# Attention and spectral mixing on one core: where x is added, and how far z runs ahead of u in the last loop

## The chip, the core and the metric

The kernel runs on one core of one Trainium2 chip. The metric is the device time of one execution in microseconds (us). A profile of one execution on the chip stands beside the times. PE is the matrix engine (PEld its weight loads), DVE the vector engine, ACT the scalar engine, POOL the GpSimd engine, SP the engine that here only issues DMAs.

## The reference

Two stages. The first is causal attention with a decay bias, for batch 8, 8 heads, sequence 576, head size 64:

```
scores = q k^T / 8 + min(-(cum_i - cum_j), 0), causal      cum = cumsum(max(s, 0))
attn   = softmax(scores);   x = attn v                      x: 8 x 576 x 512
```

The second mixes x in frequency, with 64 modes, each with its own 512 x 512 complex matrix:

```
X = rfft(x over the sequence)[:64];   Y = X (w_r + i w_i) per mode;   y = irfft(Y)
u = x + y;   z = u w_ch;   out = u + max(z, 0)              out: 8 x 576 x 512, float32
```

The mode matrices are 134 MB in float32. They are most of what the kernel reads.

## The kernel before, in words

**Schedule.** The instructions of each engine run in the order in which the program writes them (`manual_schedule`); semaphores for data and for the reuse of buffers are put in by the framework.

**First part.** A loop over 32 steps (4 groups of two heads, 8 batches) does attention, the forward transform of x and, beside it, the products with the mode matrices of group after group (128 input columns each). The mode matrices stream in by DMAs that POOL issues (line 225), 256 KB each, into two rings of buffers, throughout. The modes are cut into eight chunks of eight; `modes(g, c)` (line 443) multiplies chunk c of group g and adds it to `y_acc`.

**Last group.** After the loop the chunks of group 3 come one by one (lines 775 to 808), each making the final rows of Y for its modes. For each chunk the rows are transposed (`y_transposed`), multiplied by w_ch (`y_times_wch`), and spread over `yv`, which holds Y and Y w_ch for all chunks: chunks 0 to 3 and 4 to 5 by `gather`, chunks 6 and 7 by DMAs on SP's queue (`spread`). With `yv` there, u and z of a block of 128 rows are small matmuls with the inverse transform G: u = x + G Y and z = x w_ch + G (Y w_ch).

**Pairs.** The output goes out in 18 pairs of blocks of 128 rows by 512 columns: 16 pairs are two neighbouring blocks of one batch, and pairs 4 and 10 are tails, the last 64 rows of four batches each. x w_ch of a pair takes 8 transposes on PE (`x_transposed`, line 606), two copies on DVE and 8 matmuls (`x_times_wch`, line 618). For pairs 2 to 17 it is worked out beforehand and kept in SBUF, in one of three ways (`ways`, "esesvsesvsesvses" for pairs 2 to 17):

- "e": two float16 parts, put into z by four matmuls with the identity on PE (line 845);
- "s": float32, copied into z's PSUM buffer by ACT (line 841);
- "v": float32, added to z by DVE at the end (line 761).

Pairs 0 and 1 (`NPRE = 2`) have their x w_ch made between chunks 4 and 5 and left in z's PSUM buffers. While chunk 7 is multiplied, `modes` calls `first_u` and `first_z` between its parts: they open u of pair 0 and z of pairs 0 and 1 with the chunks that are done. When chunk 7 is there, its own part is added (`add_last`), relu is taken, and pair 1's u is made.

**Last loop.** For pair i of 2 to 17, in this order: `pre(i)` adds G (Y w_ch) into z (two matmuls of 512 columns, after the four of way "e"); `start_u(i)` puts x into u's PSUM by two matmuls with the identity (line 732); `add_y` adds G Y (two matmuls, line 713); ACT seeds z of the next pair where its way is "s"; `relu(i)` on ACT (line 751, 1024 columns); `finish(i)` adds u and relu on DVE, one add of 512 columns for each block (line 766; for way "v" lines 761 and 762), and SP issues one output DMA for each block (line 768; in tails one for 64 rows).

**PSUM.** z has two buffers of two banks. u alternates between `upool` (even pairs) and `auxpool` (odd pairs), two buffers of one bank in each.

Of the kernel before, what the change touches and what calls it, by code (L numbers as in the profile page):

```python
# [9 lines left out]
FP32 = mybir.dt.float32  # L10
# [8 lines left out]
def kernel(  # L19
# [11 lines left out]
    nc = tc.nc  # L31
# [74 lines left out]
    wpool = ctx.enter_context(tc.tile_pool(name="w_sb", bufs=WA))  # L106
    wpool2 = ctx.enter_context(tc.tile_pool(name="w2_sb", bufs=WB))
    spool = ctx.enter_context(tc.tile_pool(name="small_sb", bufs=2))
    auxpool = ctx.enter_context(tc.tile_pool(name="aux_psum", bufs=2, space=PSUM))

    at = ExitStack()
    ap_ = at.enter_context(tc.tile_pool(name="attn", bufs=1))
# [330 lines left out]
    def modes(g, c, meanwhile=None):  # L443


        ps = auxpool.tile([P, DM], FP32, name="yp", tag="aux")
        cols = xs[g % 2].rearrange("p q k h r b m -> p q k (h r b) m")

        def product(ri, q_, cg):
            k0 = HP if ri == 1 and c == 0 and cg == 0 else 0  # L450
            nc.tensor.matmul(  # L451
                ps[32 * cg : 32 * cg + 32, :],
                cols[k0:, q_, 1 - ri, :, c * MC // 2 + cg],
                wt[(g, c, ri, cg // 2)][k0:, 2 * (cg % 2) + q_, :],
                start=(ri == 0 and q_ == 0), stop=(ri == 1 and q_ == 1),
                tile_position=(k0, 32 * cg), skip_group_check=True,
            )

        for x in range(4):
            ri, y = divmod(x, 2)  # L460
            if meanwhile and x in meanwhile:
                meanwhile[x]()
            for z in range(4):
                if meanwhile:
                    product(ri, z // 2, 2 * y + z % 2)
                else:
                    product(ri, y, z)
        if g == 0:
            nc.vector.tensor_copy(out=y_acc[:, c, :], in_=ps)
# [22 lines left out]
    for i, b in ((4, 0), (10, B // 2)):  # L492
        pairs.insert(i, ((b, NF), (b + 2, NF)))
    NPRE = 2
    kept = list(range(NPRE, len(pairs)))


# [83 lines left out]
    Gx_sb = finpool.tile([P, NX, NF * P], FP16, name="Gx_sb")  # L581
    nc.vector.memset(Gx_sb.rearrange("p c t -> p (c t)").bitcast(FP32), 0.0)
    nc.sync.dma_start(out=Gx_sb[0:P:B], in_=d_Gx)
    upool = ctx.enter_context(tc.tile_pool(name="u_psum", bufs=2, space=PSUM))
    zpool = ctx.enter_context(tc.tile_pool(name="z_psum", bufs=2, space=PSUM))

    NLOC = 5
    old = xs_flat[0]
# [11 lines left out]
    def parts(b, T):  # L600

        if T < NF:
            return [(slice(0, P), b, ident16h)]
        return [(slice(NL * i, NL * i + NL), b + i, ident16h[:NL, :NL]) for i in range(2)]

    def x_transposed(i):
        xts[i] = xt_sb[len(xts) % 2]
        for x, (b, T) in enumerate(pairs[i]):
            ps = upool.tile([P, DT, P], FP32, name="xt_ps", tag="u")
            for rows, bb, ident in parts(b, T):  # L610
                for dt in range(DT):
# [92 lines left out]
    order_z = list(late)  # L704
    TAKE = (3, 2, 4, 0, 0, 0)
    us, rs = {}, {}
    GK = P - 2 * MC * NX

    def add_y(dst, i, which, rows=slice(0, P), start=False):
# [9 lines left out]
    def add_last(dst, i, yb, cols=slice(0, DM), c=NX - 1):  # L719

        for x, (b, T) in enumerate(pairs[i]):
            nc.tensor.matmul(
                dst[x][:, cols], Gx_sb[:, c, bass.ts(T, P)], yb[:, cols],
                start=False, stop=True, skip_group_check=True,
            )

    def start_u(i):
        pool, tag = ((upool, "u"), (auxpool, "aux"))[i % 2]
        us[i] = [pool.tile([P, DM], FP32, name="u_ps", tag=tag) for x in range(2)]
        for x, (b, T) in enumerate(pairs[i]):  # L730
            for r, bb, ident in parts(b, T):
                nc.tensor.matmul(  # L732
                    us[i][x][r, :].rearrange("p (g d) -> p g d", d=P), ident,
                    x_all[: r.stop - r.start, :, bb, T, :],
                    start=True, stop=False, skip_group_check=True, tile_position=(0, r.start),
                )

    def result(i):

        if i % 2 == 0 or i == len(pairs) - 1:  # L740
            return finpool.tile([P, 4 * DM], BF16, name="r_sb", tag="r", bufs=3).bitcast(FP32).rearrange(
                "p (x e) -> p x e", x=2
            )
        t = wpool.tile([P, WM, DM], BF16, name="r_w", tag="w")
        return t.rearrange("p m e -> p (m e)").bitcast(FP32).rearrange("p (x e) -> p x e", x=2)
# [6 lines left out]
                out=rs[i][:, n * x : n * x + n], in_=zs[i][:, n * x : n * x + n], func=ACTF.Relu  # L752
            )

    def finish(i):
        if ways.get(i) == "v":
            rs[i] = result(i)
        for x, (b, T) in enumerate(pairs[i]):
            o = rs[i][:, x, :]
            if ways.get(i) == "v":  # L760
                nc.vector.tensor_tensor(out=o, in0=zs[i][:, x, :], in1=z1s[i][:, x, :], op=ALU.add)
                nc.vector.scalar_tensor_tensor(
                    out=o, in0=o, scalar=0.0, in1=us[i][x], op0=ALU.max, op1=ALU.add
                )
            else:
                nc.vector.tensor_tensor(out=o, in0=us[i][x], in1=o, op=ALU.add)
            for r, bb, _ in parts(b, T):
                nc.sync.dma_start(
                    out=out[bb, bass.ds(T * P, r.stop - r.start), :], in_=rs[i][r, x, :]
                )  # L770

    def z_of(i):
        return [zs[i][:, x, :] for x in range(2)]
# [1 line left out]
    for c in range(NCK - 2):  # L775
        yb = modes(NG - 1, c)
        for x in range(TAKE[c] - 1):
            work()
        if c >= NY:
            x_transposed(c - NY)  # L780
        yt = y_transposed(yb, c)
        if TAKE[c]:
            work()
        if c >= NY:
            x_times_wch(c - NY, False)
            y_times_wch(c, yt)
            if c == NCK - 3:
                gather(NY, NCK - 2, (), (0,))
        elif c == NY - 1:
            gather(0, NY, (1, 3), (1, 0))  # L790
    assert not order_z and not ahead
    c = NCK - 2
    yb6 = modes(NG - 1, c)
    yt = y_transposed(yb6)
    vb6 = y_times_wch(c, yt)


    def first_u():
        start_u(0)
        add_y(us[0], 0, 0, slice(0, GK))  # L800
        add_last(us[0], 0, yb6, c=0)

    def first_z():
        for i in range(NPRE):
            add_y(z_of(i), i, 1, slice(0, GK))
            add_last(z_of(i), i, vb6, c=0)

    yb = modes(NG - 1, NCK - 1, {2: first_u, 3: first_z})

    yt = spool.tile([P, DT, P], FP16, name="yt_sb", tag="yt")  # L810
    for x in range(2):
# [2 lines left out]
        for dt in range(dts.start, dts.stop):  # L814
            nc.tensor.transpose(ps[:, dt - dts.start, :], yb[:, bass.ts(dt, P)], ident16h)
        nc.scalar.copy(out=yt[:, dts], in_=ps)
    add_last(us[0], 0, yb)
    vb = spool.tile([P, DM], FP16, name="v_sb", tag="v")
    for cols in halves:
        vp = auxpool.tile([P, DM // 2], FP32, name="v_ps", tag="aux")  # L820
        for dt in range(DT):
            nc.tensor.matmul(
                vp, yt[:, dt, :], wch_sb[:, dt, cols], start=(dt == 0), stop=(dt == DT - 1)
            )
        nc.vector.tensor_copy(out=vb[:, cols], in_=vp)
    spread(NCK - 1, 1, vb)
    for i in range(NPRE):
        for cols in halves:
            add_last(z_of(i), i, vb, cols)
        relu(i, 2 - i)  # L830
    start_u(1)
    add_y(us[1], 1, 0, slice(0, GK))
    add_last(us[1], 1, yb6, c=0)
    add_last(us[1], 1, yb)


    def seed(i):
# [17 lines left out]
            zs[i] = zpool.tile([P, 2, DM], FP32, name="z_ps", tag="z")  # L855
        add_y(z_of(i), i, 1, start=ways[i] == "v")

    if ways[NPRE] == "s":
        seed(NPRE)
    for i in range(NPRE):  # L860
        finish(i)
    last = len(pairs) - 1
    for i in range(NPRE, len(pairs)):
        pre(i)
        start_u(i)
        add_y(us[i], i, 0)
        if ways.get(i + 1) == "s":
            seed(i + 1)
        if ways[i] != "v":
            relu(i, 2 if i == last else 1)  # L870
        finish(i)


# [28 lines left out]
```

## Time and profile before

| | |
|---|---|
| median of 8 runs | 450.99 us (449.75 to 451.75) |
| the profiled execution | 449.75 us, span 447.9 us |
| mean granted PE clock | 0.892 |
| busy in the span: PE, DVE, ACT, POOL | 355.4, 257.3, 222.1, 241.8 us |
| DMA | 93.31 MB, 81.29 of it from POOL's queue |
| last two DVE adds of the loop | from 443.39 on, 1.28 us |

The span is from the first to the last instruction. Matmuls are pipelined: their ends are modelled, and PE being busy doesn't mean that it is at its peak. Shares of the whole span average over stages with different limits; the weight stream runs for the first nine tenths, the last loop has the last thirty microseconds or so.

### The profile page before, as it was taken

Reading aid. Unit: us, or ns where it says so; the run is one execution under the profiler, and the core shown is the slowest. Engines: PE = TensorE matmul, PEld = TensorE weight load, DVE = VectorE, ACT = ScalarE, POOL = GpSimd, SP = SyncE. Lnnn points to the kernel's source line nnn. Section 1 sums busy time; section 2 is a strip of 40 time slices with the busy share of each in tenths; the row PEclk is TensorE's granted clock in tenths of the full one; section 3 lists DMA queues with packets and bytes.
Section 4 is the critical chain, followed back from the end, with each engine's and each line's share of the span. In section 5 each row is a group of like instructions: output and inputs, shape, how many; then the busy total and the mean of one; then the engine's idle time right before and its main releaser. Section 6 shows DMA issues by size and latency. Waiting matters only on the chain.

```text
span 447.9 us, 11548 instructions
## 1 busy us (share of the span) xinstructions
PE 355.4 (79%) x4713; PEld 225.0 (50%) x4745; DVE 257.3 (57%) x599; ACT 222.1 (50%) x390; POOL 241.8 (54%) x397
## 2 busy tenths in 40 slices
PE   1789988996555989854979688789897996859995
PEld 1456666564333656633546455556564555423332
DVE  7774776675333566733446545546665565542796
ACT  1584778466233656733436443555650434231774
POOL 7866666755566666555666665566554444430000
PEclk9995999999678899969659966779997999988999
DMA  9999999999999999999999999999999999994688
GB/s 182 199 204 206 204 203 205 206 206 206 208 207 202 202 189 200 208 207 207 204 203 206 207 205 206 208 205 199 208 209 211 210 209 210 209 217 102 236 303 315
DMA packets 77540, 93.31 MB, mean 208 GB/s; under 512 B 30432, under 2 KB 40160, under 8 KB 77488
## 3 DMA queue, kind: packets, MB, share of 16 engines
q0 software_dynamic: 67984, 81.29, 105.0%
q1 hardware_dynamic: 9504, 11.29, 8.0%
q8 instruction: 37, 0.61, 0.5%
q14 instruction: 15, 0.12, 0.1%
HBM read 163.51 MB, written 9.44 MB: 386 GB/s over the span
## 4 chain that ended last, share of the span: by engine, by line
DMA 49%; PE 31%; DVE 8%; issue 5%; POOL 3%; ACT 3%; DVEq 0%; POOLq 0%; ACTq 0%
DMA w_sb<-in_moe_w_r_dram 24%; DMA w_sb<-in_moe_w_i_dram 12%; DMA k<-in_k_dram 5%; PE z_ps L622 5%; PE yp L451 5%; DMA q<-in_q_dram 3%; PE av_ps L402 3%; PE ft_ps L428 2%; PE sc_ps L373 2%; PE z_ps L713 2%; PE sc_ps L367 2%; PE u_ps L732 2%; DMA y_acc<-in_moe_w_r_dram 1%; PE tr_ps L332 1%; PE u_ps L713 1%
## 5 line engine op out<-in xcount | busy, mean ns | idle before, releaser
L381 ACT ACTIVATE p_sb<-sc_ps,cumt_sb 128x576 f16<-128x576 f32 (+1 forms) x256 | 141.8, 636 | 57.7 <-PE sc_ps L373 57.3
L225 POOL DMA_DIRECT2D w_sb<-in_moe_w_r_dram x120 | 71.8, 598 | 58.2 <-DMA w_sb<-in_moe_w_r_dram 17.1
L225 POOL DMA_DIRECT2D w_sb<-in_moe_w_i_dram x120 | 71.5, 596 | 48.5 <-DMA w_sb<-in_moe_w_i_dram 18.8
L225 POOL DMA_DIRECT2D v<-in_v_dram x72 | 51.8, 720 | 24.5 <-DMA w_sb<-in_moe_w_i_dram 7.2
L367 PE MATMUL sc_ps<-negm,ident 128*128 128x256 bf16 x256 | 55.5, 303 | 0.2
L402 PE MATMUL av_ps<-v,p_sb 128*128 128x65 f16 x1024 | 45.8, 200 | 0.0
L332 PE MATMUL tr_ps<-ident,q 64*64 64x64 bf16 x576 | 17.2, 209 | 35.3 <-DMA q<-in_q_dram 35.3
L451 PE MATMUL yp<-w_sb,xs 128*32 128x512 bf16 (+1 forms) x480 | 39.6, 425 | 6.7 <-DVE yv L682 1.9
L335 DVE COPY ktA<-tr_ps 64x576 bf16<-64x576 bf16 x32 | 24.0, 750 | 33.8 <-PE tr_ps L332 33.8
L335 DVE COPY qtA<-tr_ps 64x576 bf16<-64x576 bf16 x32 | 23.8, 743 | 32.9 <-PE tr_ps L332 32.9
L402 PEld LDWEIGHTS <-p_sb 128*128 128x128 f16 x1024 | 40.0, 102 | 5.2 <-DVE x_all L412 2.1
L373 PE MATMUL sc_ps<-qtA,ktA 65*128 65x512 bf16 (+2 forms) x192 | 37.1, 303 | 0.7 <-DMA qtA<-ncum_sb 0.7
L352 ACT ACTIVATE p<-sc_ps,cumt 128x64 f16<-128x64 f32 x32 | 10.1, 314 | 55.1 <-PE sc_ps L348 55.1
L438 DVE CAST xs<-ft_ps 64x128 bf16<-64x128 f32 x128 | 31.4, 284 | 10.2 <-PE ft_ps L428 9.7
L373 PE MATMUL sc_ps<-qtB,ktB 128*128 128x64 bf16 (+2 forms) x160 | 33.5, 313 | 3.3 <-issue 2.1
L428 PE MATMUL ft_ps<-Ff_sb,x_all 128*64 128x96 f16 (+1 forms) x640 | 34.9, 232 | 1.0 <-DVE x_all L412 1.0
L407 DVE TENSOR_REDUCE den<-av_ps 128x5 f32<-128x10 f32 x64 | 10.8, 169 | 42.7 <-PE av_ps L402 41.8
L412 DVE TENSOR_TENSOR x_all<-av_ps,rcp 128x320 f16<-128x320 f32 x64 | 31.5, 492 | 2.2
L332 PEld LDWEIGHTS <-q 64*64 64x64 bf16 x576 | 13.5, 121 | 37.6 <-DMA q<-in_q_dram 36.3
L332 PE MATMUL tr_ps<-ident,k 64*64 64x64 bf16 x576 | 17.1, 207 | 19.1 <-DVE qtB L335 10.3
L335 ACT COPY ktB<-tr_ps 64x576 bf16<-64x576 bf16 x32 | 20.3, 634 | 22.4 <-DVE ktA L335 21.3
L451 PEld LDWEIGHTS <-xs 128*32 128x32 bf16 (+1 forms) x512 | 19.3, 145 | 21.2 <-issue 11.5
(117 smaller groups left out, 555.4 us busy)
## 6 DMA issues: line engine op xcount, KB each, us to landing
w_sb<-in_moe_w_r_dram POOLq DMA_DIRECT2D x120, 256.0 KB, 8.0
w_sb<-in_moe_w_i_dram POOLq DMA_DIRECT2D x117, 256.0 KB, 8.2
q<-in_q_dram POOLq DMA_DIRECT2D x32, 144.0 KB, 7.2
k<-in_k_dram POOLq DMA_DIRECT2D x32, 144.0 KB, 7.1
v<-in_v_dram POOLq DMA_DIRECT2D x72, 64.0 KB, 6.8
out_dram<-r_sb SPq DMA_DIRECT2D x16, 256.0 KB, 2.2
out_dram<-r_w SPq DMA_DIRECT2D x16, 256.0 KB, 2.7
x_all<-in_moe_w_i_dram POOLq DMA_DIRECT2D x6, 256.0 KB, 7.2
```

What stands on the lines that cost most here:

```text
L225: nc.gpsimd.dma_start(out=dst, in_=src)
L332: nc.tensor.transpose(ps[rows, r, :], src[rows, r, :], ident16[rows, rows])
L335: copy(out=dst[n % NQ][rows, :].rearrange("d (p r) -> d p r", r=R), in_=ps[rows].rearrange("d r p -> d p r"),)
L367: nc.tensor.matmul(ps[:, bass.ds(w * S, W)], ident16, negm[:, bass.ts(r, W)], start=True, stop=False, skip_group_check=True,)
L373: nc.tensor.matmul(ps[:, c0 : c0 + i1 - i0], keys[:, w, r, :], qt[:, i0:i1], start=False, stop=True, skip_group_check=True,)
L381: nc.scalar.activation(out=pt[:, poff[x] : poff[x] + S - w * W], in_=ps[:, w * S : (w + 1) * S - w * W], func=ACTF.Exp, bias=cumt_sb[:, x, ...
L402: nc.tensor.matmul(ps[:, I, r : r + NCH], lhsT, rhs, start=(i == 0), stop=(i == len(todo) - 1), skip_group_check=True,)
L412: nc.vector.tensor_tensor(out=x_all[:, g, b, :, D * h : D * h + D], in0=ps[:, :, 1 : NCH], in1=rcp.unsqueeze(2).to_broadcast([P, NT, D]), ...
L428: nc.tensor.matmul(ps[HP * h : HP * h + HP, q_, :], x_all[:nT, g, b, T, q_::2], Ff_sb[:nT, T, 3 * HM * h : 3 * HM * (h + 1)], start=(T == ...
L438: nc.vector.tensor_copy(out=xs[g % 2][rows, :, k, h, :, b, :], in_=ps[rows, :, k * HM : (k + 2) * HM].rearrange("p q (r m) -> p q r m", r=2),)
L451: nc.tensor.matmul(ps[32 * cg : 32 * cg + 32, :], cols[k0:, q_, 1 - ri, :, c * MC // 2 + cg], wt[(g, c, ri, cg // 2)][k0:, 2 * (cg % 2) + ...
L622: nc.tensor.matmul(z[:, x, :], xts[i][:, x, dt, :], wch_sb[:, dt, :], start=(dt == 0), stop=(last and dt == DT - 1), skip_group_check=True,)
```

## The change

**Around chunks 5 to 7.** x w_ch of pair 0 is made with chunk 5 instead of 4, that of pair 1 around the transposes of chunk 6 instead of 5. The opening sums of z of pair 1 (`first_z(1)`) stand behind the v products of chunk 7 instead of in the middle of its mode products.

**Last loop.** z of pair i is followed by u of pair i - 2 (`LAG = 2`). u of a pair is one PSUM tile of two banks, one pool for even and one for odd pairs, which take the banks of the closed `upool` and `auxpool`. DVE's adds take both blocks of a pair in one instruction of 1024 columns, and one DMA carries both; only the last pair is done in halves. A "v" pair's sum with the kept product is made by DVE when its z is there. For the seven "s" pairs but the last (3, 5, 7, 9, 11, 13, 15), x does not go through PE: GpSimd adds it to relu(z) in SBUF, and `add_y` begins u.

```
+    LAG = 2
...
+    x_pool = [i for i in kept[:-1] if ways[i] == "s"]
...
     def start_u(i):
-        pool, tag = ((upool, "u"), (auxpool, "aux"))[i % 2]
-        us[i] = [pool.tile([P, DM], FP32, name="u_ps", tag=tag) for x in range(2)]
+        if upools[i % 2] is None:
+            (xt, aux)[i % 2].close()
+            upools[i % 2] = ctx.enter_context(
+                tc.tile_pool(
+                    name=f"u_psum{i % 2}", bufs=1, space=PSUM, side=("left", "right")[i % 2]
+                )
+            )
+        us[i] = upools[i % 2].tile([P, 2, DM], FP32, name="u_ps", tag="u")
+        if i in x_pool:
+            return
...
     def relu(i, parts_=1):
...
+        if i in x_pool:
+            b, T = pairs[i][0]
+            r = rs[i].rearrange("p x (g d) -> p x g d", d=P)
+            nc.gpsimd.tensor_tensor(
+                out=r, in0=r, in1=x_all[:, :, b, T : T + 2, :].rearrange("p g t d -> p t g d"), op=ALU.add
+            )
+
+    def kept_sum(i):
+        rs[i] = result(i)
+        nc.vector.tensor_tensor(out=rs[i], in0=zs[i], in1=z1s[i], op=ALU.add)
+
+    def finish(i, parts_=1):
+        n = 2 // parts_
+        for x in range(0, 2, n):
+            o, u = rs[i][:, x : x + n, :], us[i][:, x : x + n, :]
             if ways.get(i) == "v":
-                nc.vector.tensor_tensor(out=o, in0=zs[i][:, x, :], in1=z1s[i][:, x, :], op=ALU.add)
-                nc.vector.scalar_tensor_tensor(
-                    out=o, in0=o, scalar=0.0, in1=us[i][x], op0=ALU.max, op1=ALU.add
+                nc.vector.scalar_tensor_tensor(out=o, in0=o, scalar=0.0, in1=u, op0=ALU.max, op1=ALU.add)
+            else:
+                nc.vector.tensor_tensor(out=o, in0=u, in1=o, op=ALU.add)
+            b, T = pairs[i][x]
+            if T < NF:
+                nc.sync.dma_start(
+                    out=out[b, bass.ds(T * P, n * P), :].rearrange("(x p) e -> p x e", p=P), in_=o
                 )
...
-        if c >= NY:
-            x_transposed(c - NY)
+        if c == NCK - 3:
+            x_transposed(0)
         yt = y_transposed(yb, c)
...
         if c >= NY:
-            x_times_wch(c - NY, False)
+            if c == NCK - 3:
+                x_times_wch(0, False)
             y_times_wch(c, yt)
...
     yb6 = modes(NG - 1, c)
+    x_transposed(1)
     yt = y_transposed(yb6)
+    x_times_wch(1, False)
     vb6 = y_times_wch(c, yt)
...
-    yb = modes(NG - 1, NCK - 1, {2: first_u, 3: first_z})
+    yb = modes(NG - 1, NCK - 1, {2: first_u, 3: lambda: first_z(0)})
...
         nc.vector.tensor_copy(out=vb[:, cols], in_=vp)
+    first_z(1)
     spread(NCK - 1, 1, vb)
...
-    for i in range(NPRE, len(pairs)):
-        pre(i)
-        start_u(i)
-        add_y(us[i], i, 0)
-        if ways.get(i + 1) == "s":
-            seed(i + 1)
-        if ways[i] != "v":
-            relu(i, 2 if i == last else 1)
-        finish(i)
+    for i in range(NPRE, len(pairs) + LAG):
+        if i <= last:
+            pre(i)
+            if ways.get(i + 1) == "s":
+                seed(i + 1)
+            if ways[i] == "v":
+                kept_sum(i)
+            else:
+                relu(i, 2 if i == last else 1)
+        k = i - LAG
+        if k >= NPRE:
+            start_u(k)
+            add_y(u_of(k), k, 0, start=k in x_pool)
+            finish(k, 2 if k == last else 1)
```

More of the change, by code (lines that the diff above doesn't have):

```diff
@@ L108 @@
     spool = ctx.enter_context(tc.tile_pool(name="small_sb", bufs=2))
-    auxpool = ctx.enter_context(tc.tile_pool(name="aux_psum", bufs=2, space=PSUM))
+    aux = ctx.enter_context(ExitStack())
+    auxpool = aux.enter_context(tc.tile_pool(name="aux_psum", bufs=2, space=PSUM, side="right"))
     at = ExitStack()
@@ L583 @@
     nc.sync.dma_start(out=Gx_sb[0:P:B], in_=d_Gx)
-    upool = ctx.enter_context(tc.tile_pool(name="u_psum", bufs=2, space=PSUM))
     zpool = ctx.enter_context(tc.tile_pool(name="z_psum", bufs=2, space=PSUM))
+    xt = ctx.enter_context(ExitStack())
+    upool = xt.enter_context(tc.tile_pool(name="u_psum", bufs=2, space=PSUM))
     NLOC = 5
@@ L725, in add_last @@
             )
+    upools = [None, None]
     def start_u(i):
-        pool, tag = ((upool, "u"), (auxpool, "aux"))[i % 2]
-        us[i] = [pool.tile([P, DM], FP32, name="u_ps", tag=tag) for x in range(2)]
+        if upools[i % 2] is None:
[8 more added lines that the diff above has]
+            return
         for x, (b, T) in enumerate(pairs[i]):
@@ L732, in start_u @@
                 nc.tensor.matmul(
-                    us[i][x][r, :].rearrange("p (g d) -> p g d", d=P), ident,
+                    us[i][r, x, :].rearrange("p (g d) -> p g d", d=P), ident,
                     x_all[: r.stop - r.start, :, bb, T, :],
@@ L736, in start_u, with u_of @@
                 )
+    def u_of(i):
+        return [us[i][:, x, :] for x in range(2)]
     def result(i):
@@ L753, in relu @@
             )
[L755 to L759, printed above, removed]
-            if ways.get(i) == "v":
-                nc.vector.tensor_tensor(out=o, in0=zs[i][:, x, :], in1=z1s[i][:, x, :], op=ALU.add)
-                nc.vector.scalar_tensor_tensor(
-                    out=o, in0=o, scalar=0.0, in1=us[i][x], op0=ALU.max, op1=ALU.add
-                )
[L765 to L770, printed above, removed]
+        if i in x_pool:
[11 more added lines that the diff above has]
+            o, u = rs[i][:, x : x + n, :], us[i][:, x : x + n, :]
+            if ways.get(i) == "v":
+                nc.vector.scalar_tensor_tensor(out=o, in0=o, scalar=0.0, in1=u, op0=ALU.max, op1=ALU.add)
[5 more added lines that the diff above has]
+                    out=out[b, bass.ds(T * P, n * P), :].rearrange("(x p) e -> p x e", p=P), in_=o
+                )
+                continue
+            for x, (b, T) in enumerate(pairs[i][x : x + n], x):
+                for r, bb, _ in parts(b, T):
+                    nc.sync.dma_start(
+                        out=out[bb, bass.ds(T * P, r.stop - r.start), :], in_=rs[i][r, x, :]
+                    )
     def z_of(i):
@@ L799, in first_u, with first_z @@
         start_u(0)
[L800 to L806, printed above, removed]
-    yb = modes(NG - 1, NCK - 1, {2: first_u, 3: first_z})
+        add_y(u_of(0), 0, 0, slice(0, GK))
+        add_last(u_of(0), 0, yb6, c=0)
+    def first_z(i):
+        add_y(z_of(i), i, 1, slice(0, GK))
+        add_last(z_of(i), i, vb6, c=0)
+    yb = modes(NG - 1, NCK - 1, {2: first_u, 3: lambda: first_z(0)})
     yt = spool.tile([P, DT, P], FP16, name="yt_sb", tag="yt")
@@ L816 @@
         nc.scalar.copy(out=yt[:, dts], in_=ps)
-    add_last(us[0], 0, yb)
+    add_last(u_of(0), 0, yb)
     vb = spool.tile([P, DM], FP16, name="v_sb", tag="v")
@@ L831 @@
     start_u(1)
-    add_y(us[1], 1, 0, slice(0, GK))
-    add_last(us[1], 1, yb6, c=0)
-    add_last(us[1], 1, yb)
+    add_y(u_of(1), 1, 0, slice(0, GK))
+    add_last(u_of(1), 1, yb6, c=0)
+    add_last(u_of(1), 1, yb)
     def seed(i):
@@ L856, in pre @@
         add_y(z_of(i), i, 1, start=ways[i] == "v")
-    if ways[NPRE] == "s":
-        seed(NPRE)
     for i in range(NPRE):
```

## The prediction

> **What bounds the kernel now.** I read the page's slices first, then the stages around the two places of the change, then the chain, the groups and the order of time there. All times are microseconds of the profiled execution: span 447.9, 449.75 in all, against a median of 450.99 for the eight runs.
>
> Slices (mean busy share of the DMA engines in tenths, then what they moved):
>
> ```profile
> DMA  9999999999999999999999999999999999994688
> GB/s 182 199 204 206 204 203 205 206 206 206 208 207 202 202 189 200 208 207 207 204 203 206 207 205 206 208 205 199 208 209 211 210 209 210 209 217 102 236 303 315
> ```
>
> For 36 of 40 slices the weight stream fills the DMA engines. When it ends is seen in the issues of line 225 from 385 to 411 us, and in stages (columns: stretch, its length, busy time of PE, PEld, DVE, ACT, POOL, granted clock, DMA share, GB/s):
>
> ```profile
> L225 POOL DMA_DIRECT2D w_sb<-in_moe_w_i_dram x7: 592/592/592, 385.2 to 398.2; - x7
> ...
> DMA to landing us min/median/max: 10.0/10.4/11.1
> ```
> ```profile
> 395.80:399.20 3.40, 1.53 (x32) 0.85 (x31) 2.06 (x3) 1.74 (x4) 1.56 (x3) 1.00 1.14 213
> 399.20:402.60 3.40, 1.03 (x10) 0.48 (x6) 1.39 (x2) 0.79 (x2) 0.00 (x0) 0.50 1.12 223
> 402.60:406.00 3.40, 3.40 (x15) 0.93 (x14) 0.69 (x1) 0.00 (x0) 0.00 (x0) 0.50 1.11 221
> 406.00:409.40 3.40, 3.40 (x19) 1.18 (x19) 0.00 (x0) 0.00 (x0) 0.00 (x0) 0.99 0.52 98
> ```
>
> The last weight issue starts at 398.2; 10.4 to 11.1 later is 408.6 to 409.3. The last four products that need it start at 409.33: the stream and PE end together there, PE just busy enough to hide the wait. So nothing that makes PE earlier before 409.3 can move what follows.
>
> Order of time, after the last chunk and in the last loop:
>
> ```profile
> 409.33 0.65 PE L451 MATMUL yp<-w_sb,xs 128*32 128x512 bf16 x4
> ...
> 412.50 1.25 PE L722 MATMUL z_ps<-v_sb,Gx_sb 128*128 128x256 f16 x8
> ...
> 413.59 0.59 PE L732 MATMUL u_ps<-x_all,ident16h 128*128 128x512 f16 x2
> ...
> 417.88 1.29 DVE L766 TENSOR_TENSOR r_sb<-u_ps,r_sb 128x512 f32<-128x512 f32 x2 [1.20 <-ACT r_sb L751]
> ```
>
> And the output, in stages of the last loop:
>
> ```profile
> 418.50:419.50 1.00, 1.00 (x7) 0.39 (x4) 0.95 (x3) 0.97 (x2) 0.00 (x0) 1.00 0.05 20
> ...
> 423.30:425.80 2.50, 2.31 (x10) 0.87 (x9) 2.39 (x5) 1.77 (x2) 0.00 (x0) 1.00 0.87 199
> 426.00:432.50 6.50, 6.50 (x34) 2.45 (x34) 6.15 (x11) 4.71 (x5) 0.00 (x0) 1.00 1.00 384
> ...
> 442.00:446.40 4.40, 1.25 (x6) 0.39 (x4) 2.58 (x5) 1.24 (x3) 0.00 (x0) 1.00 1.03 396
> ```
>
> Three resources run nearly level: PE busy 6.50 of 6.50, DVE 6.15, DMA share 1.00 at 384 GB/s. The tail pairs (64 rows a transfer) go at 199 GB/s. Last packets end near 446.5, the span 1.4 later.
>
> **Opening: x of pairs 0 and 1, moved.** Each is 8 transposes (0.62), two DVE copies (1.29) and 8 products (1.90). Out of chunk 4 and behind chunk 6, they let the gather of chunks 4 and 5 start about 1.2 earlier (395.0 becomes 393.8) and fill PE behind chunk 6, where it did 1.03 of work in 3.40. Worth on the path: 0, since the weights still land at 409.3. If that cover were gone (a stream ending earlier) it would be worth up to 1. The spreads on SP's queue move with their chunks by 1 at most, 128 KB each inside the stream, which costs it at most 0.3.
>
> **Opening sums of pair 1, moved.** Four 512-column matmuls, 4 x 0.215 = 0.86, leave the stretch before 409.33, where they were free, and stand behind the last chunk's v products. PE is free there at about 412.25, and begins the eight last sums at 412.50, with a second wait of 0.2 among them. So 0.86 less 0.46 = 0.4 is added: x of pair 1 starts at 414.0, not 413.59. Behind it wait the relus of pairs 0 and 1, and z of pair 2: 415.3 becomes 415.7.
>
> **Fill of the lag.** Now pair 2's DVE add starts 417.88. After: z of 2 (4 x 0.215 + 2 x 0.215 = 1.29), end of pipe 0.17, relu 1.02, hand-overs 0.1 (z of 4 takes the buffer of z 2), z of 4 (0.86 + 0.55, a tail pair), u of 2 (0.86), hand-over 0.2: 5.05. The first add starts at 420.75, 2.9 later, and runs 1.22: its output is issued at 422.05, where today its halves go out at 418.59 and 419.19.
>
> **Adds of 1024 columns.** Rows (line, engine, operation; count, busy, mean ns):
>
> ```profile
> L766 DVE TENSOR_TENSOR r_w<-u_ps,r_w 128x512 f32<-128x512 f32 x16 | 10.3, 685 | 0.7 <-ACT r_w L751 0.4
> L515 DVE TENSOR_TENSOR z<-z_ps,z 128x1024 f16<-128x1024 f32 x1 | 1.2, 1225 | 1.4 <-ACT z L514 1.4
> L284 DVE TENSOR_TENSOR_SCAN p_sb<-xs,p_sb 64x576 f32<-64x576 f32 x1 | 1.3, 1349 | 0.0
> ```
>
> Ready 512-column adds follow each other at 0.605 (their 0.685 overlap by 0.08): 1.21 a pair. One of 1024 takes 1.225, so 1.145 apart. A kept pair ("v") took 2.79 from 424.34 to 427.13, and will take two such, 2.29. Sum: today 13 x 1.21 + 3 x 2.79 = 24.1 inside the 26.8 from 417.88 to 444.67; after, 15 x 1.145 + 3 x 1.145 + 1.29 (the last, in halves) = 21.9. From 420.75 DVE ends at 442.7 if never starved, and about 444 with the waits on z that I count below. ACT's 8 seeds and 13 relus (21.5) stay.
>
> **x on GpSimd.** PE loses 7 x 2 x 0.215 = 3.0 of its loop's 25.7 (14 pairs of six matmuls at 1.29, two tail pairs at 1.65, five seeds at 0.86). GpSimd does no arithmetic of size in this trace. The same shape on DVE is 1.22; the slowest elementwise row per element, the scan, is 2.34 ns an element, or 2.40 for 1024. I take 2.4, since two SBUF inputs on a slower engine are nearer to that end. With each step begun at the later of its engine and its inputs, the relus of the seven pairs come about 2.8 apart, the nearest two at 2.77, and DVE wants the sums two pairs later: at 1.22 and at 2.40 alike it is hidden, and the cover is gone at 2.8. GpSimd issues its last DMA at 398.2, so nothing is queued behind. DVE waits for GpSimd in order: a late x would hold the kept pair's sum behind it, and PE's z behind that. [...]
>
> **z two ahead.** A new wait: z of pair i+2 needs relu or kept sum of i, and u of i is queued behind it on PE. At pair 4 that is 0.85 of idle PE (in the fill above); at each kept pair z stands behind a DVE queue that is full, some 0.4 to 0.8, three times: 1.3 of DVE starvation, hence 444.
>
> **Output, what is late next.** 14 ordinary pairs of 0.524 MB at 390 GB/s are 1.34 each, 18.8; two tail pairs at 200 are 2.62 each, 5.2: 24.0 from the first packet of pair 2. The merged transfer saves SP one issue (0.33), off the path. First packet 0.9 after the issue, as at 418.59 and 419.5 today: 422.05 + 0.9 + 24.0 = 447.0. To that come gaps where a pair is finished after its predecessor has gone out; I take 0.5 (0 to 1.3). Last packet 447.5 against 446.5: **+1.0**. Span 448.9, profiled time 450.75, median **452.0**.
>
> **Rivals.**
> A. *Not slower: the output is no bound, DVE ends last.* For it: SP saves issues, and the tails' 199 GB/s may be a matter of issue (four of 0.53 to 0.59), not of the engines. If tails went at 390 the floor falls by 2.6 to 444.4, and the end is DVE's 442.7 to 444 plus the 1.8 from DVE's last add to the last packet today (444.67 to 446.5): 444.5 to 445.8, so -0.7 to -2.0, median 449.0 to 450.3. Against it: DMA share 1.00 at 384 GB/s for 6.5 us, and the late first output. It decides if the two tail pairs take less than 3.9 together. Middle 449.6.
> B. *GpSimd is the bound.* From 2.8 an add on. At half again the scan's price, 3.6 (an estimate): seven are 25.2 from 419.2 to 444.4, then three pairs' adds, 3.6, and 1.8 of output: 449.8, +3.3, median 454.3. Against: both rows.
> C. *The clock drops at the wrong time.* Above, 1.53 of PE work in 3.40 was followed by two stages at clock 0.50. After the move PE has about 1.9 of waiting between 405 and 409.3; should the granted clock halve from 409.4 on, the products, transposes, u and v there grow, as v did from 1.03 to 1.89: about +1.3, median 453.3. [...]
>
> **Numbers.** Forecast 0.48 (its own range 450.7 to 453.3), A 0.27, B 0.10, C 0.15. The range is 449.5 to 454.4: A's lower half and what exceeds B are left out. About 0.2%, 0.9 us, is what a measurement can tell from no change, so same is 450.1 to 451.9. Faster: 0.22 of A. Same: 0.05 of A, 0.17 of the forecast. Slower: 0.31 of the forecast, B and C: 0.56.
>
> **What would show it.** Last weight product still near 409.3; z of pair 2 at 415.7; first 1024-column add of the loop near 420.75, adds of 1.22 at 1.15 spacing; GpSimd adds of 2.2 to 2.5 with no DVE wait on POOL; DMA share 1.0 from 427 to the end, tails at 200 GB/s, last packet about 447.5. A first add before 419.5, or tails at 390, would make it wrong downwards; DVE waits on POOL, or a clock of 0.50 after 409.4, upwards.

## The result, and the profile after

The changed kernel took 452.5 us (median of 16 runs, 451.79 to 457.14) beside 450.54 us for the kernel before (43 runs). The ratio is 1.0051, 95% interval 1.0038 to 1.0064: slower by some 2.3 us (1.7 to 2.9); the two medians lie 2.0 apart. The forecast was 452.0, and slower. Its level is 0.5 off; its difference, +1.0, was too small by about half, and the profiles show which term was short.

Its profiled execution took 453.52 us, span 451.5, which is 3.8 above the profiled execution of before. Of these 1.1 come ahead of everything that follows: the last product with weights starts at 410.45 instead of 409.33, since it waited for its weights. In the ten profiled executions that have the changed opening it starts anywhere between 408.95 and 411.56, so one execution of each kernel can't tell whether the change has a part in this. Below, times marked "after the last weight product" are counted from that instruction's start in each kernel; for the last output packet, whose time is taken from the trace's DMA records, this gives 37.15 before and 39.63 after, +2.48.

The slices of the changed kernel, with the clock first:

```profile
PEclk9996999997585989976869698899995999989998
DMA  9999999999999999999999999999999999993588
GB/s 180 201 203 206 205 203 205 206 206 207 207 207 198 203 179 200 208 207 206 204 191 206 206 207 206 207 205 203 210 210 211 209 209 209 213 218 69 205 297 336
```

The weight stream fills 36 slices as before. The 37th carries 69 GB/s instead of 102, and nothing behind it makes that up. Order of time, from the last weight product to the first add of the loop (the bracket is what ended the engine's idle time before):

```profile
410.45 0.65 PE L452 MATMUL yp<-w_sb,xs 128*32 128x512 bf16 x4 [0.87 <-DMA w_sb<-in_moe_w_i_dram]
...
415.12 0.59 PE L746 MATMUL u_ps<-x_all,ident16h 128*128 128x512 f16 x2
...
416.85 1.03 PE L879 MATMUL z_ps<-r_sb,ident16h 128*128 128x512 f16 x4
...
419.42 1.02 PE L879 MATMUL z_ps<-r_sb,ident16h 128*128 128x512 f16 x4 [0.68 <-ACT r_sb L768]
...
422.08 1.23 DVE L790 TENSOR_TENSOR r_sb<-u_ps,r_sb 128x1024 f32<-128x1024 f32 x1 [3.71 <-PE u_ps L717]
...
423.33 0.37 SPq L793 DMA_DIRECT2D out_dram<-r_sb  x1
```

The last weight product waits 0.87 for its weights; in the kernel before it followed PE's other work without idle time. x of pair 1 follows 4.67 after it (4.26 before), z of pair 2 6.40 (5.99 before), and the first add of the loop 11.63 (8.55 before), after DVE has waited 3.71 us for u of pair 2, because z of pairs 3 and 4 stands ahead of it on PE. What the loop does then, in stages of the output (columns as in the prediction: stretch, length, busy time of PE, PEld, DVE, ACT, POOL, granted clock, DMA share, GB/s):

```profile
425.00:426.00 1.00, 1.00 (x5) 0.39 (x4) 1.00 (x2) 0.71 (x1) 0.72 (x1) 1.00 1.07 414
426.00:427.00 1.00, 1.00 (x6) 0.48 (x5) 1.00 (x2) 0.97 (x2) 0.61 (x1) 1.00 0.84 326
427.00:428.00 1.00, 1.00 (x7) 0.41 (x6) 0.85 (x2) 1.00 (x2) 1.00 (x1) 1.00 0.17 35
428.00:429.00 1.00, 1.00 (x8) 0.33 (x6) 1.00 (x1) 0.86 (x2) 0.52 (x1) 1.00 0.84 197
429.00:430.00 1.00, 1.00 (x8) 0.37 (x5) 1.00 (x2) 0.97 (x2) 0.45 (x1) 1.00 0.18 41
430.00:431.00 1.00, 0.74 (x4) 0.23 (x3) 0.33 (x1) 0.53 (x1) 1.00 (x1) 1.00 0.64 152
...
440.00:445.00 5.00, 4.44 (x21) 1.75 (x18) 4.79 (x5) 3.20 (x5) 2.14 (x1) 1.00 1.01 366
445.00:450.00 5.00, 0.21 (x1) 0.00 (x0) 1.59 (x3) 0.19 (x1) 0.00 (x0) 0.90 1.03 400
```

Pairs 2 and 3 go out at up to 414 GB/s and are all but gone by 427. Then the DMA engines stand nearly still twice, at shares 0.17 and 0.18, while the tail pair 4 goes out. From 440 on they are full, and DVE is done at 446.6, 3.5 before the last packet. The chain of waits names the tail pair and what it holds up (start, time, what):

```profile
425.68 1.02 DVE r_sb L790
...
426.72 0.54 SPq L799
...
427.31 0.58 SPq L799
...
427.94 1.70 SPq L799
...
429.68 2.43 DMA out_dram<-r_sb
...
432.13 0.05 DVEq L781
```

Pair 4's four 64-row issues follow each other on SP, the third taking 1.70 where the others took 0.54 to 0.60. Its buffer comes free at 432.1, and DVE's kept sum of pair 10, which takes that buffer, waits for it. DVE's own list of waits in the loop (total, times, longest) has little else:

```profile
DVE r_sb L790 <- PE u_ps L717: 3.7, 1, 3.7
DVE r_sb L790 <- ACT r_sb L768: 2.0, 1, 2.0
DVE r_sb L781 <- DMA out_dram<-r_sb: 1.9, 1, 1.9
DVE r_sb L788 <- PE u_ps L717: 0.2, 1, 0.2
```

3.7 is the fill of the lag, 2.0 the wait of pair 0's add ahead of the loop, 1.9 the buffer. DVE waits for POOL nowhere.

The sum, in time after the last weight product: opening +0.41; from z of pair 2 to the first add 5.23 instead of 2.56, +2.67; from that add's start to the first packet of pair 2 2.15 instead of 1.55 (one wide add and one transfer instead of halves), +0.60; from that packet to the last 25.86 instead of 27.06, -1.20. Together +2.48.

### The profile page after: what moved, and what is told of

The parts are those of the page before. It is cut to its first block, busy times and chain, and to the rows that moved or that the text cites. A ratio compares the mean times of both kernels' runs of the same rounds, so it can differ in the third digit from the quotient of the medians.

```text
span 451.5 us, 11474 instructions
## 1 busy us (share of the span) xinstructions
PE 355.9 (79%) x4699; PEld 224.9 (50%) x4731; DVE 254.8 (56%) x579; ACT 222.1 (49%) x390; POOL 256.7 (57%) x404
## 4 chain that ended last, share of the span: by engine, by line
DMA 56%; PE 27%; DVE 8%; issue 4%; ACT 1%; POOL 1%; SPq 1%; DVEq 0%; ACTq 0%
DMA w_sb<-in_moe_w_i_dram 30%; DMA w_sb<-in_moe_w_r_dram 11%; DMA q<-in_q_dram 8%; DMA k<-in_k_dram 5%; PE av_ps L403 5%; PE sc_ps L374 4%; PE ft_ps L429 4%; PE yp L452 4%; PE sc_ps L368 3%; PE tr_ps L333 3%; DVE qtB L336 2%; DVE qtA L336 1%; DVE x_all L413 1%; DMA qtA<-ncum_sb 1%; DMA xs<-c_negm 1%
## 5 line engine op out<-in xcount | busy, mean ns | idle before, releaser
L452 PE MATMUL yp<-w_sb,xs 128*32 128x512 bf16 (+1 forms) x480 | 42.6, 433 | 10.0 <-DMA w_sb<-in_moe_w_i_dram 3.6
L374 PE MATMUL sc_ps<-qtA,ktA 65*128 65x512 bf16 (+2 forms) x192 | 39.1, 315 | 0.6 <-DMA qtA<-ncum_sb 0.6
L429 PE MATMUL ft_ps<-Ff_sb,x_all 128*64 128x96 f16 (+1 forms) x640 | 33.6, 226 | 1.0 <-DVE x_all L413 1.0
L775 POOL TENSOR_TENSOR r_w<-r_w,x_all 128x1024 f32<-128x1024 f32 x7 | 14.9, 2134 | 27.8 <-ACT r_w L768 27.8
```

Source lines behind the costliest of these rows:

```text
L374: nc.tensor.matmul(ps[:, c0 : c0 + i1 - i0], keys[:, w, r, :], qt[:, i0:i1], start=False, stop=True, skip_group_check=True,)
L429: nc.tensor.matmul(ps[HP * h : HP * h + HP, q_, :], x_all[:nT, g, b, T, q_::2], Ff_sb[:nT, T, 3 * HM * h : 3 * HM * (h + 1)], start=(T == ...
L452: nc.tensor.matmul(ps[32 * cg : 32 * cg + 32, :], cols[k0:, q_, 1 - ri, :, c * MC // 2 + cg], wt[(g, c, ri, cg // 2)][k0:, 2 * (cg % 2) + ...
L775: nc.gpsimd.tensor_tensor(out=r, in0=r, in1=x_all[:, :, b, T : T + 2, :].rearrange("p g t d -> p t g d"), op=ALU.add)
```

## Experiments

The theory after the result: the time of the first output of the loop sets the end, because from there the output takes some 25 to 26 us. So the second step of the lag is the cost, and neither the opening nor GpSimd is. Rivals: the opening sums cost it, GpSimd's adds cost (or bring) something, or the result buffers do. All ratios are to the kernel before, in five rounds. The kernels were timed in several sets on different chips, each set with the kernel before beside it, so they are compared with one another through these ratios.

| kernel | median us | ratio, 95% interval |
|---|---|---|
| changed kernel | 452.5 | 1.0051 (1.0038 to 1.0064) |
| opening alone | 450.72 | 0.9996 (0.9984 to 1.0007) |
| opening sums of pair 1 back | 451.89 | 1.0032 (1.0020 to 1.0044) |
| z one pair ahead | 449.71 | 0.9979 (0.9970 to 0.9988) |
| z two ahead, x on PE | 452.39 | 1.0044 (1.0024 to 1.0064) |
| z one ahead, x on PE | 450.05 | 0.9984 (0.9972 to 0.9996) |
| z not ahead, x on PE | 450.61 | 1.0009 (0.9992 to 1.0025) |
| z one ahead, opening sums back | 449.84 | 0.9977 (0.9964 to 0.9989) |
| the same, tails on two queues | 450.02 | 0.9977 (0.9960 to 0.9994) |
| two ahead, other result buffers | 452.28 | 1.0024 (1.0007 to 1.0040) |
| lag grows from 0 to 2 | 452.04 | 1.0027 (1.0013 to 1.0042) |
| two ahead, no tail output | 450.16 | 0.9994 (0.9977 to 1.0012) |
| two ahead, GpSimd adds twice | 459.89 | 1.0199 (1.0178 to 1.0220) |

**The opening alone.** The kernel before with the moves around chunks 5 to 7 and `first_z(1)` late; the last loop as it was.

```
-        if c >= NY:
-            x_transposed(c - NY)
+        if c == NCK - 3:
+            x_transposed(0)
...
-    yb = modes(NG - 1, NCK - 1, {2: first_u, 3: first_z})
+    yb = modes(NG - 1, NCK - 1, {2: first_u, 3: lambda: first_z(0)})
...
+    first_z(1)
     spread(NCK - 1, 1, vb)
```

> The opening half of the change alone, on the kernel before: x w_ch of pairs 0 and 1 moved to chunks 5 and 6, pair 1's opening sums behind chunk 7's v products; the last loop as before. Theory L (the lag's late first output against the output transfers is what costs): only 0.4 us of the change's 2.0 lie here, so +0.4 us (ratio 1.001), with x of pair 1 starting 4.6 us after the last weight product instead of 4.2. Rival O (the opening carries it: sums late, or PE waiting before 409 and its clock): +1.5 to +2.0 us, ratio 1.003 to 1.0045.

Ratio 0.9996. In its trace x of pair 1 comes 4.67 and z of pair 2 6.40 after the last weight product, as in the changed kernel, so the 0.4 of the prediction is there; its last packet is 37.56 after, 0.4 later than in the kernel before. A change of 0.4 us is 0.1%, within the width of the interval, which ends at 1.0007, or 0.3 us: the opening by itself is not where the 2.3 us come from.

**Opening sums back.** The changed kernel with pair 1's opening sums where they were.

```
-    yb = modes(NG - 1, NCK - 1, {2: first_u, 3: lambda: first_z(0)})
+    yb = modes(NG - 1, NCK - 1, {2: first_u, 3: lambda: (first_z(0), first_z(1))})
...
-    first_z(1)
```

> The changed kernel with pair 1's opening sums back between the last mode products, as before. Theory L: 0.4 us less than the changed kernel, +1.6 against before, ratio about 1.0035. Rival O (the opening carries it): most of the loss goes, ratio 1.001 or less.

z of pair 2 comes back to 5.98, the first add to 11.21, some 0.41 earlier each, and the last packet to 38.72, 0.9 earlier. Ratio 1.0032 against 1.0051: some 0.9 us, with intervals that overlap. With z one ahead, the same edit moved the last packet of the profile by 0.4, and nothing in the time (0.9977 against 0.9979). So these sums cost 0.4 in the traces, perhaps somewhat more in the time with z two ahead, and most of the loss remains without them.

**z one pair ahead.** The changed kernel with one number changed.

```
-    LAG = 2
+    LAG = 1
```

> The changed kernel with z one pair ahead of u (LAG = 1) and all else kept. Theory L: the first add of the loop comes about 1.5 us earlier (the wait of z of pair 4 on relu and its 1.4 of matmuls leave the fill), the output ends about 1.5 earlier: +0.5 us against before, ratio about 1.001. GpSimd's 2.13 us then shows as DVE waits on POOL of up to 0.5 at some pairs, made up by the fill. Rival G (the extra work on GpSimd and the waits around it carry the loss, the lag hides it): slower than the changed kernel by 1 to 3 us, ratio 1.007 or more.

Ratio 0.9979: 3.2 us faster than the changed kernel (0.72%) and about 0.9 faster than the kernel before. The expectation had the direction and not the size: it put the gain at 1.5 and the ratio at 1.001. Its order of time at the first add of the loop:

```profile
410.11 0.65 PE L452 MATMUL yp<-w_sb,xs 128*32 128x512 bf16 x4 [0.63 <-DMA w_sb<-in_moe_w_i_dram]
...
419.37 1.22 DVE L790 TENSOR_TENSOR r_sb<-u_ps,r_sb 128x1024 f32<-128x1024 f32 x1 [1.36 <-PE u_ps L717]
```

9.26 after the last weight product instead of 11.63. The last packet is 37.16 after it instead of 39.63: 2.4 earlier at the start, 2.5 at the end. From the first packet of pair 2 to the last it takes 25.75, with two ahead 25.86. The second step of the lag thus costs its own fill and brings nothing back. That the two stretches are of one length is an observation and not a law: with z one ahead the DMA engines stand still too, but elsewhere (no output between 423 and 424, behind pair 2, and 59 GB/s between 428 and 429, behind pair 4). With the adds this near, DVE does wait for GpSimd here:

```profile
DVE r_w L790 <- POOL r_w L775: 2.5, 3, 1.6
```

and it costs no time that shows: the last packet follows DVE's last add by 3.2, and with x on PE (below) the time is the same.

**x on PE, at two, one and no pairs ahead.** `x_pool` emptied, so that GpSimd does no arithmetic and PE does 14 more products.

```
-    x_pool = [i for i in kept[:-1] if ways[i] == "s"]
+    x_pool = []
```

Two ahead:

> The changed kernel, lag of two kept, with x of the seven pairs through PE again (14 matmuls of 512 columns, 3.0 us of PE). Theory L (late first output against the output transfers): GpSimd's adds neither cost nor bring anything at this lag, 0 +- 0.4 us from the changed kernel, ratio 1.003 to 1.006 against before. Rival G (GpSimd's adds hold DVE or the pairs behind): faster than the changed kernel by 1 us or more, ratio 1.002 or less. If PE was what bound the changed loop, 2 to 3 us slower, ratio 1.009 or more.

One ahead (`LAG = 1`):

> The changed kernel with z one pair ahead of u instead of two and x of all pairs on PE, GpSimd without arithmetic. With z one ahead and GpSimd adding x the ratio was 0.998; with no distance and x on PE 1.001. If GpSimd's adds are worth what they take off PE (14 products of 0.215, 3.0 us, in a loop where PE is nearly full), this kernel is 1 to 2 us slower than the one with GpSimd, ratio 1.000 to 1.003. If the transfers set the end there too, it is within 0.4 us of it, ratio 0.997 to 0.999; the schedule says +0.3 us.

None ahead (`LAG = 0`):

> The changed kernel without lag (u of a pair directly behind its z) and with all x through PE, so what is left of the change is the opening, adds of 1024 columns and one transfer for each pair. Theory L: first add 2.7 us earlier than in the changed kernel, output end about 1.3 earlier: +0.7 us against before, ratio 1.000 to 1.002. If instead the wide adds or the merged transfers cost by themselves (an add can't start before both halves are there, a transfer leaves later): still +2 us, ratio 1.004 or more.

Two ahead 1.0044, with GpSimd 1.0051; one ahead 0.9984, with GpSimd 0.9979. The intervals overlap widely in both: taking 3.0 us of products off PE is worth nothing that can be measured, in either order. Last packet after the last weight product: 39.13 and 39.63 two ahead, 37.08 and 37.16 one ahead. None ahead, where only the 1024-column adds, the one transfer for each pair and the opening differ from the kernel before, the ratio is 1.0009, and the last packet 37.11 against 37.15 before. Between none and one ahead the times differ by 0.0025, the profiles' last packets by 0.03 us. What the first step of the lag brings, if anything, is therefore not explained by the profiles and stays open; what the second costs, 0.006 to 0.007 with x on either engine, is.

**The lag grows inside the loop.** None for pair 2, one for pairs 3 to 5, two from pair 6 on.

```
+    k = NPRE
     for i in range(NPRE, len(pairs) + LAG):
...
-        k = i - LAG
-        if k >= NPRE:
+        while k <= last and k + (0 if k == 2 else 1 if k < 6 else LAG) <= i:
...
+            k += 1
```

> The changed kernel with the distance between z and u growing inside the loop: none for pair 2, one pair for pairs 3 to 5, two from pair 6 on. If only the time of the first output counts, pair 2 goes out about 2.7 us sooner than in the changed kernel and the end follows: 2 us faster than it, ratio to the kernel before 0.998 to 1.002. Rival (a schedule I worked out from the rows, each step begun at the later of its engine and its inputs): each growth of the distance is an iteration without a finished pair, so the gap that was in front of the first output reopens behind pair 2 and pair 5, and with the DMA engines already level with PE and DVE it is not made up: 0 +-0.4 us against the changed kernel, ratio 1.004 to 1.006.

Ratio 1.0027, between the two expectations, so both were off. Its adds of pairs 2 and 3:

```profile
418.75 1.23 DVE L790 TENSOR_TENSOR r_sb<-u_ps,r_sb 128x1024 f32<-128x1024 f32 x1 [1.05 <-ACT r_sb L768]
...
422.30 1.23 DVE L790 TENSOR_TENSOR r_w<-u_ps,r_w 128x1024 f32<-128x1024 f32 x1 [2.32 <-POOL r_w L775]
```

With its last weight product at 409.81, pair 2's add comes 8.94 after it, 2.7 sooner than in the changed kernel, and pair 3's 12.49, against 12.77 there (423.22): the gap has moved behind pair 2, as the schedule said. The last packet comes 0.87 sooner all the same, and the wait of 1.9 for pair 10's buffer is not among its waits. An early first output alone is not enough, and the theory as put above fails here: from the first packet of pair 2 to the last it takes 27.7. What counts is that the pairs behind it follow.

**No tail output.** The changed kernel without the output transfers of pairs 4 and 10.

```
-            for x, (b, T) in enumerate(pairs[i][x : x + n], x):
+            for x, (b, T) in enumerate(()):
```

> The changed kernel without the output transfers of the two tail pairs 4 and 10, whose 512 rows are thus not written; all sums are made as before. If the 64-row transfers hold up the output, two times 2.4 to 3.6 us of queue go: DVE's 1.9 us wait for a buffer vanishes, the last packet follows DVE's last add by about 1.8 us instead of 3.5, and the kernel is 1.5 to 3 us faster than the changed one (ratio to the kernel before 0.998 to 1.002). Rival (rival A of the prediction): DVE and PE end last and the transfers are no bound: within 0.5 us of the changed kernel, ratio about 1.005.

Ratio 0.9994: 2.6 us faster than the changed kernel (0.57%), as expected of transfers that bound the loop. The buffer wait is gone, DVE's last add ends 34.39 after the last weight product instead of 36.14, the last packet follows 37.07 after it instead of 39.63. A stage near its end:

```profile
436.00:441.00 5.00, 4.55 (x21) 1.95 (x20) 4.83 (x5) 3.29 (x4) 3.14 (x2) 1.00 0.74 289
441.00:446.60 5.60, 1.44 (x6) 0.38 (x4) 2.90 (x4) 0.79 (x2) 0.00 (x0) 0.98 1.03 397
```

Even so the DMA engines close the loop at 397 GB/s, and the last packet follows the last add by 2.7, not by the 1.8 expected. From the first packet of pair 2 to the last it takes 23.3, where 14 pairs at 1.34 are 18.8: with the tails gone the DMA engines are not full on the way (share 0.74), and the transfers are the bound only at the end. With 1.05 MB less to write it is still no faster than the kernel with z one ahead that writes everything (0.9979).

**Other result buffers.** The results of pairs 10, 12 and 17 taken from the weight ring, so that pair 10 does not wait for pair 4's transfer.

```
-        if i % 2 == 0 or i == len(pairs) - 1:
+        if i % 2 == 0 and i not in (10, 12):
```

> The changed kernel with the results of pairs 10, 12 and 17 in three of the weight buffers, so that no result waits for an earlier pair's output to leave its buffer (the profile shows 1.9 us of DVE and 0.7 of ACT in such waits). Theory L: those waits are the output's own lateness seen from the engines; the output stays as late, 0 to 0.5 us faster than the changed kernel, ratio 1.003 to 1.005 against before. Rival R (a lag of two is too long for three result buffers, and that is the loss): 1.5 to 2 us faster, ratio 1.001 or less.

The wait of 1.9 is gone and DVE ends 34.39 after the last weight product, 1.75 earlier, the same as without tail output. But the last packet comes only 0.93 earlier (38.70), and the ratio is 1.0024, 1.2 us under the changed kernel (the intervals just overlap). That lies between the two expectations, 0 to 0.5 and 1.5 to 2. So the buffer is perhaps a part of the loss; about half of what DVE gains doesn't reach the last packet.

**Tails on two queues.** The kernel with z one ahead and the opening sums back, with one edit more: the upper halves of the tails go out through POOL's queue.

```
-                    nc.sync.dma_start(
+                    (nc.gpsimd if r.start else nc.sync).dma_start(
```

The same without that edit, on which it stands (`LAG = 1` and the edit of "opening sums back"):

> Lag of one, and pair 1's opening sums back between the last mode products. Theory: the two are independent, so 0.4 us less than lag of one alone: 449.3, ratio about 0.997, with z of pair 2 starting 6.0 us after the last weight product instead of 6.4. If the opening is hidden behind something else at this lag: 0 from lag of one alone, ratio 0.998.

And with it:

> As the kernel with a lag of one and the sums back, with the upper 64 rows of each tail transfer issued by GpSimd, so that both halves are in flight at once. If the 200 GB/s of the tail pairs come from the order of half-wide transfers in one queue: the two halves overlap, a tail pair takes 1.3 to 1.6 us of the transfers instead of 2.6, and the end comes 0.5 to 1.5 us earlier, ratio 0.994 to 0.996. If the 64-row transfers are slow in themselves whatever runs beside them: no gain, or up to 0.5 lost to GpSimd's issues, ratio 0.997 to 0.998.

Both have ratio 0.9977. In the profiles the last packet is 0.54 sooner with two queues (36.22 against 36.76), and no issue on SP takes longer than 0.60, where one of pair 5 takes 1.78 with one queue; in the time it does not show, though the intervals would hide 0.5 us. 0.9977 is what the second of its expectations gave: no gain.

The first of the two, z one ahead with the opening sums back, and the kernel that only sets `LAG = 1` are the fastest here: 449.84 and 449.71 us, both under the kernel before (the intervals of the ratio end at 0.9989 and 0.9988) and under the changed one.

**GpSimd adds twice.** The same add made a second time in each of the seven pairs.

```
+            for _ in range(2):
                 nc.gpsimd.tensor_tensor(
...
                 )
```

> The changed kernel with GpSimd's add made twice in each of the seven pairs (x is thus added twice there): 4.25 us of GpSimd a pair instead of 2.13. The prediction put the end of the cover at 2.8 us an add; by the schedule, 4.25 makes GpSimd the bound and gives +5 to +8 us against the changed kernel (ratio to the kernel before 1.015 to 1.023), with waits of DVE on GpSimd at most of the seven pairs. Rival: the adds have more room than that (the transfers set the end), and the time moves by less than 2 us (ratio below 1.009).

Ratio 1.0199 (four runs), 1.48% above the changed kernel, 6.7 us: inside the 5 to 8 expected. POOL's group, its stage in the loop, and DVE's waits:

```profile
L776 POOL TENSOR_TENSOR r_w<-r_w,x_all 128x1024 f32<-128x1024 f32 x14 | 29.5, 2127 | 22.8 <-ACT r_w L768 22.2
```
```profile
435.00:440.00 5.00, 4.14 (x21) 1.55 (x21) 4.19 (x5) 2.75 (x3) 4.92 (x3) 1.00 0.77 297
```
```profile
DVE r_w L791 <- POOL r_w L776: 8.7, 7, 1.9
```

POOL is busy 4.92 of 5.00 and DVE waits for it at all seven pairs. So the cover that the prediction named is real and ends between 2.13 and 4.25 us an add; where in between (2.8 was worked out) was not tried.

## Why the prediction was right, and where it was short

**Opening: right.** The last weight product waits for its weights (0.87) after the moves of x, and the opening alone gave 0.9996, so they are worth nothing that can be measured; the opening sums cost 0.41 where 0.4 was worked out.

**Fill of the lag: right.** The first add was put 11.42 after the last weight product (420.75 less 409.33) and came at 11.63; the first packet of pair 2 at 13.6, and it came at 13.78. The experiment with z one ahead shows that this step carries the loss.

**Adds of 1024 columns: right in size.** 1.22 each and 1.13 to 1.14 apart:

```profile
L790 DVE TENSOR_TENSOR r_w<-u_ps,r_w 128x1024 f32<-128x1024 f32 x8 | 9.7, 1216 | 0.0
```

**DVE's end: wrong by its wait.** 444 was forecast in the time of before, 34.7 after the last weight product; it was 36.14. The 1.3 of starvation was put to z standing behind the kept sums on DVE, three times. Those waits did not come: beside the fill and the buffer, 0.2 is all. In their place DVE waited once, 1.9, at kept pair 10, for the buffer that the tail pair 4 was still going out of. The prediction counted the wait for z at that sum but not the reuse of its result buffer.

**x on GpSimd: right.** Taken at 2.40, measured at 2.13 (DVE's adds of 1024 columns took 1.22), hidden:

```profile
L775 POOL TENSOR_TENSOR r_w<-r_w,x_all 128x1024 f32<-128x1024 f32 x7 | 14.9, 2134 | 27.8 <-ACT r_w L768 27.8
```

Adding x on DVE was not tried: x was put back on PE alone, and the time stayed the same (1.0044 beside 1.0051).

**Output: the term that was mis-sized.** The forecast had the DMA engines full from 427 on; they were not, and this is the step that fell short. The floor of 24.0 us from the first packet of pair 2 was right in kind: in the kernels with wide adds and all their output it takes 24.9 to 26.0 (27.7 where the lag grows and the gap lies behind pair 2, 32.4 where GpSimd is made the bound). But the gaps on top were taken at 0.5 and are 1.9 (25.86 less 24.0). Nearly all of it lies at pair 4. The four stages from 427 to 431 shown above moved 0.43 MB (35, 197, 41 and 152 KB) in 4.0 us, where 200 GB/s would take 2.1. Two things lie there in the trace. DVE's kept sum of pair 6, which the lag moves ahead of pair 4's add, holds that add from 424.35 to 425.48, so that pairs 2 and 3 are gone before pair 4 follows:

```profile
424.35 1.22 DVE L781 TENSOR_TENSOR r_sb<-z_ps,z 128x1024 f32<-128x1024 f32 x1
...
425.48 1.22 DVE L790 TENSOR_TENSOR r_sb<-u_ps,r_sb 128x1024 f32<-128x1024 f32 x1
```

And one of pair 4's issues takes 1.70 on SP. What each is worth by itself was not tried. Two profiles with z two ahead point to the issue: where it took 1.19 (opening sums back) and 1.05 (x on PE), the output took 25.37 and 25.38 instead of 25.86. With the other result buffers it took 24.9 beside an issue of 1.72, so a gap at pair 4 can also be made up in part behind it. The prediction had the second tail right: it went at 202 GB/s.

```profile
438.00:440.00 2.00, 1.59 (x8) 0.68 (x7) 2.00 (x3) 1.27 (x2) 1.68 (x1) 1.00 0.85 202
```

With gaps of 1.9 in place of 0.5, the prediction's +1.0 becomes +2.4, which is what the traces (+2.48) and the ratio (+1.7 to +2.9) give. That the forecast's level is off by only 0.5 is in part luck: it was set on the 450.99 of the eight runs before, and beside the changed kernel the kernel before took 450.54, so a base 0.45 too high made up for a part of what the term was short.

**Rivals.** A, that the output is no bound, fell: the tails did not go at 390 GB/s, the last packet follows DVE's end by 3.5, and leaving out their output gave 2.6 us. B, GpSimd as the bound, is what the doubled add shows, at 4.25 an add and not at 2.13. C, the clock, did not come in the changed kernel's profile (granted clock 1.00 in every stage from 409 to 430), but it came in one other:

```profile
411.00:412.00 1.00, 1.00 (x6) 0.41 (x5) 0.00 (x0) 0.54 (x2) 0.00 (x0) 0.53 0.00 0
412.00:413.00 1.00, 1.00 (x6) 0.68 (x5) 0.17 (x1) 0.00 (x0) 0.00 (x0) 0.50 0.46 131
413.00:414.00 1.00, 1.00 (x6) 0.57 (x4) 0.57 (x2) 0.00 (x0) 0.00 (x0) 0.50 0.00 0
```

This is the kernel with the doubled adds, whose instructions up to here are those of the changed kernel. In its profiled execution z of pair 2 started 8.07 after the last weight product instead of 6.40: the mechanism of C, at 1.67 where 1.3 was worked out, in one of the ten profiled executions that have this opening. So up to 1.67 of that kernel's 6.7 may be the clock's; the waits on POOL are there all the same.

## What to carry to other kernels

Where the transfers of a loop are level with its engines, as in the kernel before (DMA share 1.00 and PE busy 6.50 of 6.50 us from 426 to 432.5), a software pipeline's fill may not be paid back. Here the second pair of lead delayed the loop's first add by 2.4 us and the last packet by 2.5; the first pair of lead delayed the add by only 0.3 and cost nothing. Count the lag in time ahead of the first output, take the least that covers the wait (here one pair, not two), and when a result buffer is reused, set the next writer against the landing of the slowest transfer out of it (here DVE waited 1.9 us for it), not against the engine that filled it.

## What the runs showed of the hardware that was not expected

A 128 KB output issue of 64 rows on SP's queue usually took 0.53 to 0.60 us. But in the profiles of eleven of the twelve kernels whose tails all go out through SP's queue, one output issue at the first tail or just behind it took 1.05 to 1.82: 1.70 at pair 4 in the changed kernel, 1.82 at pair 5 with z one ahead, 1.27 with the opening alone, whose loop is that of the kernel before. In the twelfth, the kernel before, none took over 0.59. The four issues of the first tail, before and in the changed kernel:

```profile
422.17 2.45 SPq L768 DMA_DIRECT2D out_dram<-r_sb  x4
```
```profile
426.72 3.56 SPq L799 DMA_DIRECT2D out_dram<-r_sb  x4
```

None took over 0.60 with the tails on two queues, and none over 0.51 without tail output. In some kernels later issues were long as well: the last of the changed kernel took 1.10, and with the other result buffers eleven of the 25 took over 0.7. So neither the wide adds nor the lag nor GpSimd's arithmetic is needed for a long issue (with x on PE it was 1.05 two ahead, 1.22 one ahead). What makes the issue long is open.
